# Moving the load of query 0's first 24 keys from SyncE's DMA queue to ScalarE's in a decode attention and GLU kernel

## The chip, the cores and the metric

One core of one Trainium2 chip. The metric is the device time of one execution in microseconds (us); the kernel before took 1301.58 us (median of three runs, 1301.52 to 1301.68). All data is float32.

## The reference, cut to what matters

```python
B, Sq, D = 2, 1, 448;  H, Sk, Dh = 16, 8192, 256;  F = 1792
q = (layernorm(x) @ wq).reshape(B, Sq, H, Dh).transpose(0, 2, 1, 3)
scores = einsum("bhqd,bhkd->bhqk", q, k_cache) * Dh ** -0.5
o = einsum("bhqk,bhkd->bhqd", softmax(scores), v_cache)
h = x + o.transpose(0, 2, 1, 3).reshape(B, Sq, H * Dh) @ wo
n = layernorm(h)
out = h + ((n @ w_gate) * (n @ w_up)) @ w_down
```

There is one new token for each of two batch rows, and 16 heads, so 32 queries; each has its own 8192 keys and 8192 values of 256 numbers, 8 MB each. The caches are some 537 MB of the 561 MB that the kernel reads: each byte of them is used once.

## The kernel before, in words

**Tiles.** A query's 8192 keys lie as 128 partitions by 64 keys by 256 numbers; a partition's 64 keys are 64 KB in one piece of memory. One buffer, `k_sb`, holds 2 x 64 - 16 = 112 keys a partition: even queries use its keys 0 to 63, odd ones 48 to 111 (`k_base`, line 276), so that 16 keys are shared ground. `v_sb` holds one query's values (64 a partition).

**Scores on VectorE.** `scores` (line 451) multiplies a part of the keys by the query, spread over all partitions, with one `tensor_mul` in place in `k_sb`, and sums over the 256 numbers with one `tensor_reduce`. Query 0 comes in two parts (`FIRST`, line 22): first the keys 40 to 63 of each partition, 24 of them, then the keys 0 to 39. The product of query 0's first part alone is written to `v_sb` instead of in place (lines 458 and 459). So keys 48 to 63 of `k_sb`, which query 1's keys overwrite, are free as soon as that product is done, and `v_sb` is free for query 0's values when its reduction is done. Queries after that take a part of 16 keys and one of 48.

**The rest of a query.** `top` and `softmax` take the largest score, the exponentials (ScalarE) and their sum; `mix` multiplies the values by the probabilities on TensorE as they land, and the results run through `wo` into `acc_ps`. After 32 queries come the second layernorm and the GLU, whose weights are loaded over `k_sb`.

**The start.** ScalarE issues the load of x (line 264) on its own DMA queue. SyncE issues all other loads of the kernel on its queue, in program order: the weights of the first head pair (`load_w`, line 303, 896 KB), the 24 keys (3072 KB) and the 40 keys (5120 KB) of query 0 (lines 304 and 305). Then, inside the loop over queries from line 612 on: query 1's keys (8192 KB), which wait for the product of the 24 keys; query 0's values, which wait for the reduction of the 24 keys; query 2's keys, which wait for query 1's first part; the next weights, and so on, keys and values in turn. VectorE and TensorE meanwhile do the layernorm of x, and TensorE then computes the first two heads' queries for both batch rows from the first weights (lines 389 to 402): four groups of four matmuls, each copied by ScalarE into `qs`. The first group is what query 0 needs.

**How orders and waits arise.** `Orders` collects the instructions of each engine in the order of the program. `load` (line 163) and `put` work out for each what it has to wait for, from the regions read and written, and `write` (line 201) emits the waits (`wait_ge`) and the instruction, with a semaphore that counts it. An engine runs its list in order, so a load that waits holds up the loads behind it on the same engine. In the profile, line 176 is that of every load, 229 that of every compute instruction, and 183 a wait of TensorE's.

Of the kernel before, what the change touches and what calls it, by code (L numbers as in the profile page):

```python
# [16 lines left out]
NJ = SK // P  # L17
# [4 lines left out]
FIRST = ((NJ - AHEAD, NJ), (0, NJ - AHEAD))  # L22
# [193 lines left out]
def decode_block(nc, x, k_cache, v_cache, w, wg, wu, wd, out):  # L216
# [31 lines left out]
    buffers = {"k": k_sb, "v": v_sb}  # L248
# [17 lines left out]
    def keys(cache, i, lo, hi):  # L266
        h, b = divmod(i, B)
        return cache[b, h].rearrange("(p j) d -> p j d", p=P)[:, lo:hi, :]

    def load_keys(name, cache, i, lo, hi, buf, at, event=None):  # L270
        o.load(
            "SP", name, buffers[buf][:, at : at + hi - lo, :], keys(cache, i, lo, hi),
            writes=[(buf, at * DH, (at + hi - lo) * DH)], event=event,
        )

    def k_base(i):
        return i % 2 * (NJ - OVER)

    def load_k(i, lo=0, hi=NJ):
        load_keys(f"d_k_{i}_{lo}", k_cache, i, lo, hi, "k", k_base(i) + lo)  # L280

    def v_parts(i):
        got, lo = [], 0
# [6 lines left out]
    def load_v(i, part):  # L290
        lo, hi, buf, at = part
        load_keys(f"d_v_{i}_{lo}", v_cache, i, lo, hi, buf, at, "e_v" if i < LOOP else None)

    def load_w(name, k, lo, hi, event=None):
        o.load("SP", name, w_sb[:, lo:hi], w[k][:, lo:hi], writes=[("w", lo, hi)], event=event)
# [5 lines left out]
        return 2 * WQ + h % 4 * WO  # L301

    load_w("d_w0", 0, 0, WQ)
    for lo, hi in FIRST:
        load_k(0, lo, hi)

    ident = sb("ident", P, P)
    put("POOL", "memset", ident, 0.0, w=["ident"])
# [77 lines left out]
    def q_at(h):  # L386
        return h % 2 * (1 + h // 2 % 2)

    for k in range(2):
        for b in range(B):  # L390
            for c in range(DC):
                at = c * 2 * DH + (k * DH if c < DC - 1 else 0)
# [5 lines left out]
            at = q_at(k)  # L398
# [213 lines left out]
    for n in range(NQ + 1):  # L612
        hp, at = divmod(n, 2 * B)
# [11 lines left out]
        if n + 1 < NQ:  # L625
            load_k(n + 1)
        for part in parts[1:]:
            load_v(n - 1, part)
        if n % 8 == 1:
            k = n // 8 + 1  # L630
# [35 lines left out]
    at = 0  # L666
# [191 lines left out]
```

## Time and profile before

| what | value |
|---|---|
| time, median of three runs | 1301.58 us |
| span of the profiled execution, first to last instruction | 1300.5 us |
| what lies around the span, against that median | 1.1 us |
| VectorE busy | 1130.8 us, 87% |
| TensorE busy | 488.8 us, 38% |
| ScalarE busy | 62.6 us, 5% |

The profiled execution has no time of its own listed beside its span; 1.1 us is the median less the span.

In the rows of the timeline the columns are start and duration in us, the engine, the line in the kernel, the operation, what it writes and reads, how many instructions are merged in the row, and in brackets the idle time before it and what ended that. A row with SPq or ACTq is the issue of a load by SyncE or ScalarE: its duration is that of the issue, not of the transfer. The list of DMA issues gives for each load its size and the time from its issue to its landing. In the list of DMA queues, q1 carries what SyncE issued, and q10 what ScalarE issued (x, the only load of that engine).

### The profile page before, as it was taken

The numbers are of one execution on the slowest core, as the hardware profiler recorded it, in microseconds if no ns is written. First come the engines' busy times: TensorE is split into PE (matmuls) and PEld (weight loads), VectorE is DVE, ScalarE is ACT, GpSimd is POOL, SyncE is SP. The second block draws the span as 40 slices with busy tenths as digits, with TensorE's granted clock in tenths as the row PEclk, the third lists the DMA queues.
The fourth block names the chain that finished last, engine by engine and source line by source line (L and its number), as shares of the span: only waits on it lengthen the run. The fifth ranks groups of instructions, "written<-read, shape, count | busy, mean of one in ns | idle before, by whom it ended". The sixth has DMA issues, their size and how long they took to land.

```text
span 1300.5 us, 6955 instructions
## 1 busy us (share of the span) xinstructions
PE 488.8 (38%) x2972; PEld 168.9 (13%) x2972; DVE 1130.8 (87%) x275; ACT 62.6 (5%) x184; POOL 1.4 (0%) x9
## 2 busy tenths in 40 slices
PE   3035422363331633215343063432424334243368
PEld 2011100120100201002101021010111001010113
DVE  7996988888988689888889868898888897889991
ACT  1000000000000000000000000000000000000000
POOL 0000000000000000000000000000000000000000
PEclk8566756686656766558666576665766667666578
DMA  9999999999999999999999999999999999999998
GB/s 414 423 434 448 424 437 431 427 441 423 448 424 435 448 423 443 427 439 429 435 435 423 433 448 423 448 424 443 427 443 427 423 436 445 426 438 429 435 433 374
DMA packets 12111, 561.45 MB, mean 432 GB/s; under 512 B 1602, under 2 KB 1732, under 8 KB 1988
## 3 DMA queue, kind: packets, MB, share of 16 engines
q1 hardware_dynamic: 12096, 561.30, 99.8%
q8 instruction: 6, 0.10, 0.0%
q14 instruction: 5, 0.04, 0.0%
q10 hardware_dynamic: 4, 0.00, 0.0%
HBM read 561.19 MB, written 0.11 MB: 432 GB/s over the span
## 4 chain that ended last, share of the span: by engine, by line
DMA 70%; DVE 29%; PE 0%; issue 0%; SPq 0%
DMA k_sb<-in_A_k_cache_dram 68%; DVE k_sb L229 14%; DVE s L229 14%; DMA k_sb<-in_wd_dram 2%; DVE nm L229 0%; PE y_ps L229 0%; SPq L176 0%; DVE m L229 0%; PE sm L229 0%; DVE v_sb L229 0%; DVE rl L229 0%
## 5 line engine op out<-in xcount | busy, mean ns | idle before, releaser
L229 DVE TENSOR_TENSOR k_sb<-k_sb,q 128x12288 f32<-128x12288 f32 (+2 forms) x67 | 549.6, 8203 | 130.3 <-DMA k_sb<-in_A_k_cache_dram 130.3
L229 DVE TENSOR_REDUCE s<-k_sb 128x48 f32<-128x12288 f32 (+2 forms) x67 | 549.3, 8198 | 0.2
L229 PE MATMUL o_ps<-v_sb,p 128*2 128x512 f32 x2000 | 288.2, 739 | 397.7 <-PEq L183 387.6
L229 PEld LDWEIGHTS o_ps<-v_sb,p 128*2 128x2 f32 x2000 | 53.7, 97 | 603.8 <-issue 591.3
L229 PE MATMUL sm<-nm,ones 1*128 1x1 f32 x64 | 16.6, 326 | 191.7 <-PEq L183 175.1
L229 PE MATMUL sm<-ident,m 128*1 128x128 f32 x32 | 10.9, 341 | 137.0 <-PEq L183 106.1
L229 PE MATMUL q_ps<-w_sb,xb 128*128 128x256 f32 (+1 forms) x172 | 59.3, 503 | 0.0
L229 ACT ACTIVATE o_sb<-o_ps 128x512 f32<-128x512 f32 x32 | 19.1, 597 | 703.9 <-PE o_ps L229 703.9
L229 PE MATMUL sm<-sel,o_sb 128*128 128x1 f32 x256 | 33.7, 253 | 25.8 <-PEq L183 22.9
L229 PE MATMUL acc_ps<-w_sb,oT 128*2 128x448 f32 x60 | 36.6, 749 | 15.9 <-PEq L183 11.0
L229 PEld LDWEIGHTS sm<-nm,ones 1*128 1x128 f32 x64 | 14.6, 283 | 201.2 <-issue 183.5
L229 PEld LDWEIGHTS sm<-sel,o_sb 128*128 128x128 f32 x256 | 31.8, 195 | 55.6 <-issue 48.2
L229 PEld LDWEIGHTS q_ps<-w_sb,xb 128*128 128x128 f32 x172 | 33.7, 200 | 30.0 <-issue 27.6
L229 PE MATMUL sm<-lsum,ones 128*128 128x1 f32 x64 | 17.5, 342 | 26.0 <-PEq L183 23.1
L229 ACT ACTIVATE nb<-sm 128x1 f32<-128x1 f32 x32 | 5.5, 171 | 395.7 <-PE sm L229 395.7
L229 PEld LDWEIGHTS sm<-ident,m 128*1 128x1 f32 x32 | 2.6, 81 | 149.8 <-issue 115.3
L229 PEld LDWEIGHTS sm<-lsum,ones 128*128 128x128 f32 x64 | 15.6, 303 | 28.0 <-issue 24.7
L229 ACT ACTIVATE q<-q_ps,rstd 128x512 f32<-128x512 f32 (+1 forms) x18 | 11.5, 640 | 71.9 <-PE q_ps L229 71.9
L229 PE MATMUL o_ps<-k_sb,p 128*2 128x512 f32 x48 | 9.3, 934 | 6.1 <-DMA k_sb<-in_A_v_cache_dram 6.1
L229 ACT ACTIVATE p<-s,nb 128x64 f32<-128x64 f32 x32 | 11.1, 347 | 1.0
L229 DVE TENSOR_TENSOR v_sb<-k_sb,q 128x6144 f32<-128x6144 f32 x1 | 6.6, 6557 | 4.8 <-DMA k_sb<-in_A_k_cache_dram 4.8
L229 PE MATMUL q_ps<-k_sb,xr 128*32 128x256 f32 (+3 forms) x96 | 10.0, 506 | 1.6 <-DMA k_sb<-in_B_w_gate_dram 1.6
(79 smaller groups left out, 85.1 us busy)
## 6 DMA issues: line engine op xcount, KB each, us to landing
v_sb<-in_A_v_cache_dram SPq DMA_DIRECT2D x4, 4096.0 KB, 30.5
w_sb<-in_w_dram SPq DMA_DIRECT2D x3, 3584.0 KB, 37.8
v_sb<-in_A_v_cache_dram SPq DMA_DIRECT2D x1, 6144.0 KB, 24.3
k_sb<-in_A_k_cache_dram SPq DMA_DIRECT2D x1, 5120.0 KB, 24.6
v_sb<-in_A_v_cache_dram SPq DMA_DIRECT2D x2, 2048.0 KB, 27.3
k_sb<-in_A_v_cache_dram SPq DMA_DIRECT2D x1, 4096.0 KB, 35.3
k_sb<-in_B_w_gate_dram SPq DMA_DIRECT2D x1, 3136.0 KB, 32.4
k_sb<-in_A_k_cache_dram SPq DMA_DIRECT2D x1, 3072.0 KB, 11.6
```

Of the source, the lines that this page charges most:

```text
L229: o.put(engine, lambda: f(*args, **kw), r, w, mark, event)
```

## The change

The load of the 24 keys is issued by ScalarE, right behind the load of x and ahead of everything else on that engine; the load of the 40 keys stays on SyncE's queue, now right behind the first weights. All waits, regions and sizes stay as they were, and so do all other loads.

```diff
-    def load_keys(name, cache, i, lo, hi, buf, at, event=None):
+    def load_keys(name, cache, i, lo, hi, buf, at, event=None, by="SP"):
         o.load(
-            "SP", name, buffers[buf][:, at : at + hi - lo, :], keys(cache, i, lo, hi),
+            by, name, buffers[buf][:, at : at + hi - lo, :], keys(cache, i, lo, hi),
             writes=[(buf, at * DH, (at + hi - lo) * DH)], event=event,
         )
...
-    def load_k(i, lo=0, hi=NJ):
-        load_keys(f"d_k_{i}_{lo}", k_cache, i, lo, hi, "k", k_base(i) + lo)
+    def load_k(i, lo=0, hi=NJ, by="SP"):
+        load_keys(f"d_k_{i}_{lo}", k_cache, i, lo, hi, "k", k_base(i) + lo, by=by)
...
     load_w("d_w0", 0, 0, WQ)
-    for lo, hi in FIRST:
-        load_k(0, lo, hi)
+    load_k(0, *FIRST[0], by="ACT")
+    load_k(0, *FIRST[1])
```

## The prediction

> **What bounds the kernel now.** I read the page first: busy shares, DMA queues, the chain's summary.
>
> ```profile
> span 1300.5 us, 6955 instructions
> ...
> q1 hardware_dynamic: 12096, 561.30, 99.8%
> ...
> q10 hardware_dynamic: 4, 0.00, 0.0%
> ...
> DMA 70%; DVE 29%; PE 0%; issue 0%; SPq 0%
> ```
>
> The last row puts 70% of the chain on DMA and 29% on VectorE, but the queue row decides: SyncE's packets occupy the 16 DMA engines for 99.8% of the span. The DMA engines are the bound; VectorE appears in the chain because a load is issued when VectorE frees a buffer, while older loads still keep the engines busy. The table by stretches gives the rate, and the start.
>
> ```profile
> core 0: us, PE busy (x) PEld busy (x) DVE busy (x) ACT busy (x) POOL busy (x), PEclk, DMA share, GB/s
> 1.00:2.00 1.00, 0.00 (x0) 0.00 (x0) 0.48 (x4) 0.70 (x1) 0.84 (x4) 1.00 0.55 90
> 2.00:3.00 1.00, 0.01 (x1) 0.01 (x1) 0.88 (x3) 0.58 (x1) 0.14 (x1) 1.00 0.71 165
> 100.00:300.00 200.00, 77.82 (x437) 26.61 (x437) 173.15 (x36) 10.11 (x29) 0.00 (x0) 0.67 1.01 435
> ```
>
> A steady stretch moves 435 GB/s at a share of 1.01. So a change to the order of loads can gain only what is idle in the first 3 us, and can lose only by letting the engines run dry. The question is whether anything in the first 60 us makes a load come too late for that. Here is the timeline of that stretch.
>
> ```profile
> 0.73 0.53 ACTq L176 DMA_DIRECT2D v_sb<-in_A_x_dram  x1
> ...
> 0.73 0.38 SPq L176 DMA_DIRECT2D w_sb<-in_w_dram  x1
> ...
> 1.17 18.57 SPq L176 DMA_DIRECT2D k_sb<-in_A_k_cache_dram  x3
> ...
> 1.30 1.28 ACT L229 ACT_TABLE_LOAD   x1 [1.30 <-PEq L839]
> ...
> 7.30 9.25 PE L229 MATMUL q_ps<-w_sb,xb 128*128 128x256 f32 x32
> ...
> 11.10 0.47 ACT L229 ACTIVATE q<-q_ps,rstd 128x256 f32<-128x256 f32 x1 [1.85 <-PE q_ps L229]
> 12.83 6.56 DVE L229 TENSOR_TENSOR v_sb<-k_sb,q 128x6144 f32<-128x6144 f32 x1 [4.83 <-DMA k_sb<-in_A_k_cache_dram]
> ...
> 19.42 6.55 DVE L229 TENSOR_REDUCE s<-v_sb 128x24 f32<-128x6144 f32 x1
> 26.07 0.33 SPq L176 DMA_DIRECT2D v_sb<-in_A_v_cache_dram  x1
> 26.24 10.82 DVE L229 TENSOR_TENSOR k_sb<-k_sb,q 128x10240 f32<-128x10240 f32 x1 [0.27 <-DMA k_sb<-in_A_k_cache_dram]
> ...
> 57.05 0.33 SPq L176 DMA_DIRECT2D k_sb<-in_A_k_cache_dram  x1
> ```
>
> The DMA issues of the same stretch (size, us to landing), then one line of the view of the key buffer for the first 30 us, then an issue from the kernel's end:
>
> ```profile
> k_sb<-in_A_k_cache_dram SPq DMA_DIRECT2D x1, 5120.0 KB, 24.6
> ...
> k_sb<-in_A_k_cache_dram SPq DMA_DIRECT2D x1, 3072.0 KB, 11.6
> w_sb<-in_w_dram SPq DMA_DIRECT2D x1, 896.0 KB, 4.8
> ...
> v_sb<-in_A_v_cache_dram SPq DMA_DIRECT2D x1, 38.8
> ```
>
> ```profile
> L176 SPq DMA_DIRECT2D k_sb<-in_A_k_cache_dram x3: 328/422/423, 1.2 to 19.4; - x3
> ```
>
> ```profile
> out_dram<-v_sb SPq DMA_DIRECT2D x1, 56.0 KB, 1.6
> ```
>
> Landings: the first weights at 0.73 + 4.8 = 5.5, the 24 keys at 1.17 + 11.6 = 12.8. VectorE starts their product at 12.83; the query was ready at 11.10 + 0.47 = 11.57, so the keys were last. The product ends at 19.4, and there query 1's keys are issued, the third of the three issues. The reduction ends at 26.0, where query 0's values are issued and the 40 keys are needed; those land at about 26.2.
>
> **What the change moves.** One issue leaves SyncE: it took up to 0.42 us there (the issues of 1.2 to 19.4 took 328 to 423 ns). The 40 keys are issued at 1.17 in its place, some 0.45 us sooner; worth nothing, since their bytes stand behind the first weights. On ScalarE the new issue follows x: 0.73 + 0.53 + a step of 0.06 as on SyncE (0.73 + 0.38 to 1.17), so at about 1.3, and ends by 1.8. What it delays there is the table load of 1.28 us at 1.30, now ending near 3.1; ScalarE's next work is an activation on the variance behind TensorE's small sums, just ahead of 7.30. Cost nothing, with 4 us of cover.
>
> The real effect: the 24 keys no longer stand behind the first weights, but share the engines with whatever SyncE has queued. The bytes are the same. Engines began at about 1.45 (share 0.55 of the second microsecond), 0.7 us after the first issue; so the 24 keys' first bytes come at 1.3 + 0.7 = 2.0. By then the weights have moved 90 GB/s x 1 us = 0.09 of 0.92 MB: seven of the eight rows that each engine carries (128 rows, 16 engines) are still to go.
>
> How two queues share an engine is shown nowhere before: q10 carries four packets. I bound it. Row times: the 24 keys' 3072 KB took 12.8 - 5.5 = 7.3 us, so a 24 KB row takes 0.91 us of its engine, a 7 KB row of weights 0.27, a 40 KB row 1.51. If the engine takes the two queues row about, the weights' seven rows each wait for a row of keys: they land at 5.5 + 7 x 0.91 = 11.9, and the keys at 12.8 to 14.3 (the same bytes before them, and at most one 40 KB row). If the first weights went whole, and the keys then alternated with the 40 KB rows, they would land at 5.5 + 8 x (0.91 + 1.51) = 24.9, or one 40 KB row less, 23.4. I take row about with the weights, because seven rows are left at 2.0.
>
> Then the query comes last, not the keys: TensorE took 11.57 - 7.30 = 4.3 us from its first matmul to the query's copy, and now begins at 11.9 instead of 7.30. Query 0's first product starts at T = 16.2, later by d = 3.4 us than 12.83.
>
> What d costs. (1) Query 1's keys are issued at T + 6.6. The engines have work until the 40 keys are through: 12.8 + 12.1 (5120 KB at 435 GB/s) = 24.9 as a landing, less the time between last byte and landing. The output's 56 KB took 1.6 us in all, 0.7 of it before the first byte and 0.1 for the bytes, which leaves 0.8; so they run dry at 24.1. With 0.7 us from issue to first byte, the issue must come by 23.4, so T by 16.8 and d by 4.0: the cost is **d - 4.0 us, and nothing below that**. A d of 3.4 fits with 0.6 us to spare. As engines don't end together (the 40 keys land 1.3 us past 24.9), the early ones may lose some tenths; I take 0.1.
>
> (2) VectorE itself runs d - 0.27 late from 26.24 on (it waited 0.27 there). Query 2's keys go out at 57.05 + 3.1 = 60.2; query 0's values keep the engines busy until 26.07 + 38.8 = 64.9, less 0.8: 3.2 us to spare after 0.7 for the first byte. (3) What is left of the delay is waited out further on:
>
> ```profile
> 84.17 4.43 DVE L229 TENSOR_TENSOR k_sb<-k_sb,q 128x4096 f32<-128x4096 f32 x1 [1.04 <-DMA k_sb<-in_A_k_cache_dram]
> ...
> 131.25 4.43 DVE L229 TENSOR_TENSOR k_sb<-k_sb,q 128x4096 f32<-128x4096 f32 x1 [12.04 <-DMA k_sb<-in_A_k_cache_dram]
> ```
>
> VectorE takes back 1.04 us at 84.17 and the rest in the 12.04 us in front of 131.25, where it waits for a transfer in any case. From there on nothing differs.
>
> A gain is bounded too: between 1 and 3 us the engines are busy for 0.55 and 0.71 of the time, and the third microsecond moves 165 instead of 435 GB/s. A second queue could fill part of that from 2.0 on: (435 - 165) / 435 = 0.6 us at most. So the sum for this edit lies between -0.6 and the rivals' bounds below, and I take +0.1: 1300.6 against the span of 1300.5, which is 1301.7 on the median's scale (the 1.1 us around the span are not touched).
>
> [...]
>
> **The rivals.** *Order unchanged.* An engine finishes its whole share of a load before it turns to the other queue: weights, the 24 keys, the 40 keys, as before; T = 12.83 and 1301.6. For it: each load has nine packets on an engine (12096 packets over SyncE's 84 loads are 144, so 128 rows and one more on each of 16 engines), which may go as a unit; no row here shows two queues at work. [...]
>
> *Equal bytes.* Engines share finely: the 24 keys get half of 435 GB/s and land at 2.0 + 14.5 + 0.8 = 17.3. The weights land early, so T = 17.3, d = 4.5, cost 0.5 us, up to 1.1 for engines that end early: 1302.1 to 1302.7.
>
> *The 24 keys lose to the 40* (slower). If the weights are mostly through, because the second issue on ScalarE starts late or its queue is served late, the 24 keys alternate with 40 KB rows: landing 23.4 to 24.9, d = 10.6 to 12.1, cost 6.6 to 8.1: 1308 to 1310. If all the 40 KB rows go first, T = 26.2, d = 13.4, and 1311. It decides from a cost of 2.6 us, so d = 6.6 and T = 19.4: that takes (19.4 - 12.8) / 1.51 = 4.4 such rows ahead of the keys' last one. Against it: the two issues lie 0.6 us apart, and seven of the weights' rows are left. A table load of 1.28 us ahead of the issue would still leave about five.
>
> **How the numbers follow.** Row about: 0.54, 1301.7. Order unchanged: 0.11. Equal bytes or a few more 40 KB rows, costs of 0.5 to 2.6 us: 0.17. Keys behind the 40: 0.16. Something faster than the bound of 0.6 allows: 0.02. A measurement of this kernel tells 0.2%, 2.6 us, from no change; so faster 0.02, same 0.82, slower 0.16. The range runs from the largest gain, 1301.0, to 1304.2, which takes in the first three cases.
>
> **What would show it.** In the changed profile: ACTq with a second issue at about 1.3; TensorE's first matmul on the weights near 12 instead of 7.30; VectorE's first product near 16, the issue of query 1's keys near 23; the reduction's end near 29 and VectorE a few us late until its long wait ahead of 131; landings from then on as before. If the first product starts at 12.8, the order is unchanged; at 17 to 18 with matmuls from 7.3, bytes are shared. It is wrong if that product starts past 19 and the DMA row shows a hole near 25.

## The result, and the profile after

The changed kernel takes 1312.28 us (median of five runs, 1312.08 to 1313.19) against 1301.52 (1301.33 to 1301.68): a ratio of 1.0084, 95% interval 1.0073 to 1.0094, so 10.8 us slower. The prediction was no change, 1301.7 in a range of 1301.0 to 1304.2: wrong. What came is its slower rival, "the 24 keys lose to the 40", priced at 1308 to 1311.

From the page of the changed kernel: the span, the DMA share in 40 slices, and two queues (packets, MB, share of the 16 engines' span).

```profile
span 1311.9 us, 6955 instructions
...
DMA  6999999999999999999999999999999999999998
...
q1 hardware_dynamic: 11952, 558.16, 98.4%
q10 hardware_dynamic: 148, 3.15, 0.6%
```

All that is lost lies in the first slice, a 6 where there was a 9. ScalarE's queue now carries 148 packets: the four of x and 144 of the 24 keys. The start's timeline in the changed kernel, then its DMA issues of the first 60 us:

```profile
1.17 32.55 SPq L176 DMA_DIRECT2D k_sb<-in_A_k_cache_dram  x2
1.32 0.36 ACTq L176 DMA_DIRECT2D k_sb<-in_A_k_cache_dram  x1
...
1.71 1.28 ACT L229 ACT_TABLE_LOAD   x1 [1.71 <-PEq L839]
...
7.28 9.46 PE L229 MATMUL q_ps<-w_sb,xb 128*128 128x256 f32 x32
...
26.80 6.56 DVE L229 TENSOR_TENSOR v_sb<-k_sb,q 128x6144 f32<-128x6144 f32 x1 [18.82 <-DMA k_sb<-in_A_k_cache_dram]
...
40.04 0.33 SPq L176 DMA_DIRECT2D v_sb<-in_A_v_cache_dram  x1
...
70.66 0.33 SPq L176 DMA_DIRECT2D k_sb<-in_A_k_cache_dram  x1
```

```profile
k_sb<-in_A_k_cache_dram SPq DMA_DIRECT2D x1, 5120.0 KB, 25.3
k_sb<-in_A_k_cache_dram ACTq DMA_DIRECT2D x1, 3072.0 KB, 25.4
w_sb<-in_w_dram SPq DMA_DIRECT2D x1, 896.0 KB, 4.9
...
k_sb<-in_A_k_cache_dram SPq DMA_DIRECT2D x1, 21.8
```

The second issue on ScalarE comes at 1.32, as forecast. But the first weights still land at 0.73 + 4.9 = 5.6, and TensorE starts on them at 7.28 as before: they did not share with the keys. The 24 keys land at 1.32 + 25.4 = 26.7 instead of 12.8, and query 0's first product starts 14.0 us late. Below is which queue moved what, for 2.0 to 5.6 us, then for 6 to 6.9 and for 6.9 to 8.4, then for 6 to 24 us as a whole. A row is one partition's piece of a load. Each row is one packet here, counted in the stretch in which it starts. Each load but the tiny one of x has one more packet, of under 512 B, on each of the 16 DMA engines (144 packets for the 128 rows of the 24 keys); it is read here as the signal that the load has landed there, since in the kernel a load counts its semaphore up by 16.

```profile
q1 hardware_dynamic: 149, 1.49, 103.7%
```

```profile
q10 hardware_dynamic: 16, 0.39, 101.3%
```

```profile
q1 hardware_dynamic: 16, 0.66, 100.9%
```

```profile
q1 hardware_dynamic: 116, 4.59, 58.9%
q10 hardware_dynamic: 131, 3.12, 40.4%
```

Between 2.0 and 5.6 us nothing of ScalarE's queue moves, though the keys were issued at 1.32: SyncE's 149 packets are the rest of the weights' rows, their 16 signals, and one 40 KB row on each engine. The 24 keys' first rows start at 6.0 to 6.8, when these are done. From then on each of the 16 engines takes one row of each queue in turn: sixteen rows of 24 KB (0.39 MB), sixteen of 40 KB (0.66 MB), and so on, some 112 of 40 KB and 127 of 24 KB up to 24 us. It is row about, but with the wrong partner. At 24.5 us fifteen engines are through with both loads; the sixteenth still has a row of the 24 keys, from 25.1 to 26.0, and the landing at 26.7 waits for it. Here is all that starts between 24.5 and 34.3 us:

```profile
q10 hardware_dynamic: 2, 0.02, 0.6%
q1 hardware_dynamic: 1, 0.00, 0.0%
```

So the engines run dry, as the table by stretches shows, first of the kernel before, then of the changed one:

```profile
25.00:33.00 8.00, 0.00 (x0) 0.00 (x0) 7.73 (x2) 0.00 (x0) 0.00 (x0) 0.50 0.93 401
...
40.00:1290.00 1250.00, 469.22 (x2758) 154.71 (x2762) 1097.93 (x247) 57.36 (x176) 0.00 (x0) 0.65 1.00 433
```

```profile
25.00:33.00 8.00, 0.00 (x0) 0.00 (x0) 6.20 (x1) 0.00 (x0) 0.00 (x0) 0.50 0.01 3
...
40.00:1290.00 1250.00, 459.92 (x2675) 151.07 (x2675) 1109.08 (x235) 56.51 (x173) 0.00 (x0) 0.65 1.00 434
```

Between 25 and 33 us DMA is busy for 0.01 of the time (3 GB/s instead of 401): both loads of query 0 are through but for that one row, and query 1's keys can't be issued before the late product has ended at 33.4. From 40 us on the two kernels move the same 433 to 434 GB/s. The loss is that one hole.

### The profile page after: what moved, and what is told of

Same layout as the page of the kernel before. It is cut to its first block, busy times and chain, and to the rows that moved or that the text cites. A ratio compares the mean times of both kernels' runs of the same rounds, so it can differ in the third digit from the quotient of the medians.

```text
span 1311.9 us, 6955 instructions
## 1 busy us (share of the span) xinstructions
PE 488.6 (37%) x2972; PEld 170.2 (13%) x2972; DVE 1130.6 (86%) x275; ACT 62.7 (5%) x184; POOL 1.4 (0%) x9
## 4 chain that ended last, share of the span: by engine, by line
DMA 68%; DVE 32%; PE 0%; issue 0%; ACTq 0%; SPq 0%; DVEq 0%
DMA k_sb<-in_A_k_cache_dram 65%; DVE s L229 16%; DVE k_sb L229 15%; DMA k_sb<-in_wd_dram 2%; DVE v_sb L229 1%; DVE nm L229 0%; PE y_ps L229 0%; DVE m L229 0%; ACTq L176 0%; DVE rl L229 0%; PE sm L229 0%; SPq L176 0%; DVEq L209 0%
## 5 line engine op out<-in xcount | busy, mean ns | idle before, releaser
L229 PE MATMUL o_ps<-v_sb,p 128*2 128x512 f32 x2000 | 291.6, 745 | 391.5 <-PEq L183 381.3
L229 PE MATMUL sm<-sel,o_sb 128*128 128x1 f32 x256 | 33.7, 253 | 25.8 <-PEq L183 22.9
L229 PE MATMUL acc_ps<-w_sb,oT 128*2 128x448 f32 x60 | 34.5, 712 | 15.7 <-PEq L183 10.9
L229 PEld LDWEIGHTS sm<-lsum,ones 128*128 128x128 f32 x64 | 15.9, 308 | 28.0 <-issue 24.7
L229 ACT ACTIVATE oT<-sm,rl 128x2 f32<-128x2 f32 x32 | 8.4, 262 | 39.1 <-PE sm L229 39.1
## 6 DMA issues: line engine op xcount, KB each, us to landing
v_sb<-in_A_v_cache_dram SPq DMA_DIRECT2D x2, 2048.0 KB, 26.2
k_sb<-in_A_k_cache_dram ACTq DMA_DIRECT2D x1, 3072.0 KB, 25.4
```

Source lines behind the costliest of these rows:

```text
L229: o.put(engine, lambda: f(*args, **kw), r, w, mark, event)
```

## The experiments

Two questions: why the 24 keys ran with the 40 keys and not with the weights, and whether their lateness alone costs the 10.8 us. T is the start of query 0's first product, d its delay against 12.83. Three theories of the sharing went into the first four runs: **taken ahead** (an engine commits itself to rows in order of arrival, about ten ahead of the one it moves, an estimate from the changed kernel, where seven rows of weights, their signal and a 40 KB row went ahead of the 24 keys; only rows beyond that go in turn), **late queue** (ScalarE's queue is served late or after SyncE's), and the prediction's **row about from arrival**. The edits of these four are against the changed kernel.

**Keys first.** x goes to the head of SyncE's queue, so that the 24 keys are ScalarE's first issue.

```diff
-    o.load("ACT", "d_x", x_sb[:, :D], ...
+    o.load("SP", "d_x", x_sb[:, :D], ...
```

> The load of x goes to the head of SyncE's queue, and the load of the 24 keys is the first issue of ScalarE, at 0.73 us. Theory 'taken ahead' (each DMA engine takes rows in order of arrival, about ten ahead of those it moves, and only rows not yet taken go in turn between the queues): the eight rows of the 24 keys are all taken before the first weights arrive some 0.4 us later, so the keys land near 1.4 + 8 x 0.91 + 0.8 = 9.5 and the weights after them near 11.8; query 0's first product starts near 16 (the query comes last), a delay of 3.3 us against the kernel before, which costs nothing: 1301.5, at most 1302.5. Theory 'late queue' (ScalarE's queue is served late or behind SyncE's): weights at 5 to 6, keys in turn with the 40 KB rows, first product at 24 to 27, 1308 to 1312. Theory 'row about from arrival' (the prediction's): weights and keys both land near 12, first product near 16, 1301.5 to 1302.

Measured: 1303.05 (ratio 1.0013, 1.0003 to 1.0023). The DMA issues, then the first product:

```profile
k_sb<-in_A_k_cache_dram ACTq DMA_DIRECT2D x1, 3072.0 KB, 11.2
w_sb<-in_w_dram SPq DMA_DIRECT2D x1, 896.0 KB, 11.3
```

```profile
16.67 6.56 DVE L229 TENSOR_TENSOR v_sb<-k_sb,q 128x6144 f32<-128x6144 f32 x1 [8.67 <-ACT q L229]
```

The keys land at 0.73 + 11.2 = 11.9 and the weights, issued at 1.14, at 12.4: the two share, and the query comes last, at T = 16.67. That is the picture the prediction drew for the changed kernel, had by 0.4 us of order of arrival. "Late queue" falls here: ScalarE's rows run ahead. But "taken ahead" is too large at ten rows: all eight key rows would have landed by 9.5. Only the first three on each engine ran alone: between 1.9 and 4.5 us one completion packet was all that SyncE's queue got through. Then the two go row about, 80 packets against 79 from 4.7 to 10.8 us. The time is above what either theory had (1301.5 to 1302.5): a d of 3.84 us, under the prediction's cover of 4.0, costs 1.6 us.

```profile
q10 hardware_dynamic: 41, 1.01, 99.4%
q1 hardware_dynamic: 1, 0.00, 0.0%
```

**Both on ScalarE.**

```diff
-    load_k(0, *FIRST[1])
+    load_k(0, *FIRST[1], by="ACT")
```

> Both key loads of query 0 are issued by ScalarE behind x, the 24 keys first; SyncE keeps the rest. 'Taken ahead': weights at 5.5, 24 keys at 12.8 to 13, first product at 12.8 to 13; query 1's keys, issued by SyncE near 19.5, find the last rows of the 40 keys already taken, so the 40 keys land near 26 and the time is 1301.5 (at most 1302). 'Row about from arrival': weights near 11.9, first product near 16; query 1's 64 KB rows go in turn with the last rows of the 40 keys from about 23 on, 40 keys at 27 to 30, 1301.5 to 1303. 'Late queue': first 24-key row not before 5.7, first product near 13.8, and the 40 keys behind query 1's keys: landing at 35 or later, VectorE some 9 us or more late, 1304 or more.

Measured: 1303.04 (1301.5 to 1303.8; ratio 1.0010, 1.0000 to 1.0020). The interval doesn't tell this from no change; the profiled execution is the one of 1303.80 us. T is 12.78, against 12.83 in the kernel before: one queue behind the other's weights kept the old order, and ScalarE's queue was as good as SyncE's. But the 40 keys are needed at 25.9 and land only at 30.9, as the bracket shows; they share their last rows with query 1's keys, which SyncE issued at 19.37.

```profile
30.88 10.83 DVE L229 TENSOR_TENSOR k_sb<-k_sb,q 128x10240 f32<-128x10240 f32 x1 [4.95 <-DMA k_sb<-in_A_k_cache_dram]
```

VectorE is late by 4.6 us at query 2's keys (issued at 61.68 instead of 57.05), and the engines run short there: 1.31 between 62 and 64 us and 0.68 between 64 and 68 in this profile, 0.89 in the mean. "Taken ahead" in the strength of ten rows (landing near 26) falls again. "Row about from arrival" comes near in this landing (27 to 30), but falls by T, which it put near 16.

**Forty wait.** SyncE issues the 40 keys only when the first weights have landed.

```diff
-    load_k(0, *FIRST[1])
+    load_k(0, *FIRST[1], after=[("w", 0, WQ)])
...
```

The lines left out hand `after`, a new argument, to the load as what it reads, so that its issue waits for the landing of the weights.

> As the changed kernel, but SyncE waits for the landing of the first weights (about 5.5) before it issues the 40 keys. 'Taken ahead': the weights land at 5.5, the 24 keys' rows are all taken by then and move first; 24 keys at 12.8 to 13.5, first product at the same time, 1301.5 to 1302. 'Late queue': the 24 keys' first row comes near 5.7 and the 40 keys arrive near 6.2, then in turn: 24 keys at 21 to 25, 1306 to 1311. 'Row about from arrival': the weights land near 11.7 and only then are the 40 keys issued; the 24 keys land near 12.5, first product near 16, 1301.5 to 1302.

Measured: 1305.02 (ratio 1.0027, 1.0017 to 1.0038), T = 18.66: no theory's number. The 40 keys go out at 5.26. Three stretches of this run tell what happened, 5.9 to 9.0 us, 15.9 to 17.7 us and 17.75 to 18.25 us:

```profile
q10 hardware_dynamic: 48, 1.18, 88.3%
```

```profile
q1 hardware_dynamic: 16, 0.66, 84.1%
```

```profile
q1 hardware_dynamic: 16, 0.66, 302.8%
q10 hardware_dynamic: 16, 0.00, 1.8%
```

No row of the 40 keys starts before 9.0, 3.8 us after their issue; from 5.9 on each engine starts three more 24 KB rows first. So rows are taken ahead, but three of 24 KB, not ten. The second and third stretch are a surprise: the last rows of the 24 keys have started by 15.8 and end by 16.7, and what is left of ScalarE's queue are 16 packets of under 512 B, one for each engine, the signals of its landing. One 40 KB row on each engine (16 packets, 0.66 MB) goes ahead of them; the next sixteen start right behind them. The signal stood in line like a row, and the keys counted as landed only at 1.30 + 17.3 = 18.6, 1.9 us after the last row's end.

**Swap.** The 24 keys back on SyncE, the 40 on ScalarE.

```diff
-    load_k(0, *FIRST[0], by="ACT")
-    load_k(0, *FIRST[1])
+    load_k(0, *FIRST[0])
+    load_k(0, *FIRST[1], by="ACT")
```

> The 24 keys go back to SyncE's queue behind the first weights, and the 40 keys are issued by ScalarE behind x instead. 'Taken ahead', with rows in turn between the two queues whichever of them is ScalarE's: weights at 5.5, then one or two rows of the 24 keys ahead and the rest in turn with 40 KB rows: 24 keys near 23 to 24, first product near 23.5, a delay of 10.7 us, 1308 to 1309. 'Late queue': the 24 keys run ahead of all that ScalarE has issued and land at 12.8 as in the kernel before, 1301.5. 'Row about from arrival': the weights in turn with 40 KB rows, landing near 16; the 24 keys later than 23, 1308 to 1311.

Measured: 1312.32 (ratio 1.0083, 1.0066 to 1.0100), T = 26.39: the changed kernel's loss with the engines' roles exchanged.

```profile
26.39 6.56 DVE L229 TENSOR_TENSOR v_sb<-k_sb,q 128x6144 f32<-128x6144 f32 x1 [18.40 <-DMA k_sb<-in_A_k_cache_dram]
```

So it isn't ScalarE's queue; it is that the two loads stand on two queues at all. The size was low by 3 us. About half of it is the signal's place in the line, which was not in it: the 24 keys' rows end by 23.0, and a 40 KB row goes ahead of the signal on each engine, up to 24.5. The rest is mostly one engine, whose signal comes 1.3 us after the others', at 25.8.

The next three runs test the price of lateness, and a look-ahead put, from the runs so far, at 2.2 to 2.9 us of transfers in place of ten rows.

**Late by 14, one queue.** The kernel before, with fills by VectorE ahead of the first product.

```diff
     act(std, std, AF.Exp, scale=0.0, r=["std"], w=["std"])
+    for _ in range(3):
+        dve("memset", v_sb[:, :23, :], 0.0, w=[("v", 0, 23 * DH)])
```

> The kernel before, all loads on SyncE, with three fills of v_sb by VectorE (5888 numbers a partition each, some 6.2 us) put ahead of query 0's first product: nothing but that product is late, to about 26.6. Theory 'hole' (the loss is only that query 1's keys are issued too late, so that the DMA engines run dry from about 24 to 34): the same loss as the changed kernel at the same start, delay less 2.8 us: 1312 for a start at 26.6, with DMA idle from 25 to 33. Rival 'sharing costs' (two queues at work lose bandwidth on the engines): clearly less, 1306 or below, since only one queue is used.

Measured: 1312.64 (ratio 1.0086, 1.0069 to 1.0103). The product, and DMA in the stretch of the hole:

```profile
26.73 6.56 DVE L229 TENSOR_TENSOR v_sb<-k_sb,q 128x6144 f32<-128x6144 f32 x1
```

```profile
25.00:33.00 8.00, 1.65 (x2) 0.08 (x2) 7.89 (x3) 0.00 (x0) 0.00 (x0) 0.50 0.01 2
```

With all loads on SyncE and in the old order, the same late product makes the same hole and the same loss. Two queues at work cost no bandwidth that shows (429 GB/s from 6 to 24 us in the changed kernel, 431 in the kernel before); the late start is all of it. Here all 16 engines send the 40 keys' signal between 23.8 and 24.4. Query 1's keys are issued at 33.31, and their first rows, one on each engine, start at 34.3 to 35.0. The stretch from 34.2 to 35.2 us:

```profile
q1 hardware_dynamic: 16, 1.05, 304.5%
```

Sixteen packets that fill 304.5% of 1 us on 16 engines took 3.05 us in the mean; in the kernel before, where these rows follow others without a gap, one of 64 KB takes 2.42 (32 of them fill 107.5% of 28 to 32.5 us).

**Late by 3.** One fill, of 29 keys' room.

```diff
     act(std, std, AF.Exp, scale=0.0, r=["std"], w=["std"])
+    dve("memset", v_sb[:, :29, :], 0.0, w=[("v", 0, 29 * DH)])
```

> As the one above with one fill of 7424 numbers (some 7.8 us), so that query 0's first product starts near 15.9, 3.1 us late. Theory 'hole' with the threshold read from the runs so far (cost = delay - 2.8): 0.2 to 0.5 us, 1301.5 to 1302. With the prediction's threshold of 4.0: no change, 1301.4. If any delay of VectorE cost in full: 1304.5.

Measured: 1301.84 (ratio 1.0003, 0.9994 to 1.0013) with T = 16.08: +0.4 us, no difference that this comparison tells from none, and in the middle of the 0.2 to 0.5 expected. Costs against the kernel before in the same comparison, by d:

| run | T, us | d, us | cost, us | d - cost |
|---|---|---|---|---|
| late by 3 | 16.08 | 3.25 | 0.4 | 2.8 |
| keys first | 16.67 | 3.84 | 1.6 | 2.2 |
| forty wait | 18.66 | 5.83 | 3.6 | 2.2 |
| swap | 26.39 | 13.56 | 10.9 | 2.7 |
| late by 14 | 26.73 | 13.90 | 11.2 | 2.7 |
| changed | 26.80 | 13.97 | 10.8 | 3.2 |

Whatever made the product late in these six runs, the time grew by its delay less 2.2 to 3.2 us. The small costs are less sure than the large: that of "late by 3" lies within the noise.

**Forty late.** The changed kernel, with the 40 keys issued only when ScalarE's activation on `std` has ended.

```diff
-    load_k(0, *FIRST[1])
...
     act(std, std, AF.Exp, scale=0.0, r=["std"], w=["std"])
+    load_k(0, *FIRST[1], after=["std"])
```

> As the changed kernel, but SyncE issues the 40 keys only behind ScalarE's activation that ends near 9.25 (the second on std). Theory 'taken ahead', with about 2.2 to 2.9 us of transfers taken ahead on each engine: at 9.9, when the 40 keys arrive, the 24 keys' last 2.1 us are already taken; they land at 12.8 to 13, first product at 12.8 to 13, no hole since the 40 keys' rows are there before 12: 1301.5. Rival 'rows in turn from arrival': two or three rows of 24 keys are left at 9.9, each behind a 40 KB row: 24 keys at 15.5 to 17.5, 1301.5 to 1303.

Measured: 1302.11 (1301.51 to 1302.78; ratio 1.0006, 0.9996 to 1.0015), T = 12.85. The 40 keys' issue, then the product:

```profile
9.27 10.49 SPq L176 DMA_DIRECT2D k_sb<-in_A_k_cache_dram  x2
```

```profile
12.85 6.56 DVE L229 TENSOR_TENSOR v_sb<-k_sb,q 128x6144 f32<-128x6144 f32 x1 [4.86 <-DMA k_sb<-in_A_k_cache_dram]
```

The 24 keys are still on ScalarE's queue, the 40 on SyncE's, and 10 of the 10.8 us are back, only because the 40 keys arrive when the other load's last 2 us have been taken. In turn from arrival was expected to give a T of 15.5 or more. The profiled execution is the one of 1301.51 us; T in the others is not known. A fixed delay of whichever queue comes second, the other reading of the runs so far, doesn't fit: the 40 keys' first row starts 2.5 us after its issue here and 3.8 us in "forty wait", each time behind the rows that were in line. So in these runs the look-ahead decided which loads went in turn. No run here is faster than the kernel before; its engines, with SyncE's packets on them for 99.8% of the span, have no hole to fill.

## Why the prediction was wrong

**The step that failed** is "I take row about with the weights, because seven rows are left at 2.0". Seven rows of weights had not moved by then, but the engines had already taken them, and one 40 KB row behind them. So the 24 keys' first row came at 6.0 instead of 2.0, and the partner in the turns was the 40 keys: 1.51 us a turn instead of 0.27. The prediction weighed the count of rows not yet moved; what counted is how much stood in line at arrival. Where another load was in line, the first row of the second queue's load started 3.4 to 4.7 us after its issue, against 1.0 us for the first weights, which had an idle engine: 3.4 in "keys first" (the weights, issued at 1.14, had no row under way by 4.5), 3.8 in "forty wait" (24 KB rows ahead), 4.7 in the changed kernel (the weights' rows and a 40 KB row); 2.5 in "forty late", where only some 2 us of the other load were left. Less that 1.0, and that last run aside, some 2.4 to 3.7 us of transfers were taken ahead. In rows of one engine that is three in "forty wait" and some nine in the changed kernel, so it was no fixed number of rows; whether bytes or time set it was not tried apart.

**Row about** itself was right: between 6.0 and 8.4 us of the changed kernel sixteen rows of 24 KB start, one for each engine, then sixteen of 40 KB. The rival "order unchanged", with a whole load as the unit, is refuted by the same rows.

**The landing** of a load was taken as its last byte plus 0.8 us. In the kernel before it is 0.4 for the 24 keys (last row's end at 12.4, landing at 12.8). With a second queue at work it came later: 1.9 us in "forty wait", where a 40 KB row of the other queue started on each engine ahead of the signal.

**The cost of lateness** was right in kind (the delay less a cover, by query 1's late issue) and its cover of 4.0 us too large: 2.2 to 3.2. The time at which the engines run dry, 24.1, was right (23.8 to 24.4 in "late by 14"). Two other terms were not. From issue to first byte the sum has 0.7 us, read from the share of the second microsecond; but in the kernel before no packet starts before 1.6, and the first weights' rows start 1.0 us after their issue. Query 1's keys took 0.95 to 1.6 us after the hole. And a first row took 3.05 us in the mean after the hole of "late by 14" instead of 2.42, which the sum doesn't have. 4.0 less 0.3 to 0.9, less 0.6, is 2.5 to 3.1.

**The spread of the engines.** The prediction put the 40 keys' landing, 1.3 us past its sum, down to engines that don't end together. It is one engine alone: in the kernel before, fifteen send the 40 keys' signal by 24.5 us and the last at 25.7. In the seven runs in which a packet of 16 KB of another queue (q8, "instruction", some 0.9 us) starts between 21 and 23 us, one engine is 1.0 to 1.6 us behind the rest; where that packet comes after the 40 keys' last rows have started ("keys first", 23.8, and "late by 14", 27.7), all end within 0.6 us. That the packet holds up that engine is read from these times; no run moves it on purpose.

**Right were** the issue at 1.3, the table load's free delay (1.30 to 1.71, nothing late behind it), that no gain was to be had, and that nothing is lost after the start (434 GB/s from 40 us on). The second check, at query 2's keys, did no harm in the changed kernel, where the hole had moved query 0's values back as well; it is the one that cost in "both on ScalarE", where the cover was short too.

The rival's price came near, in part by luck: row about with 40 KB rows from the weights' end gave 23.4 to 24.9 for the landing, "all of the 40 first" 26.2 and 1311. Fifteen engines ran as the first of these has it, with eight 40 KB rows ahead of the last 24 KB row, and sent their signals by 24.5. The landing came at 26.7 because of the sixteenth engine, and the time at 1312.28 because the cover was shorter too. The rival was given 0.16, on the strength of the seven rows.

## What to carry to other kernels

In these runs one queue kept its order, and on it a small load that must land first was safe behind the loads that it needs and ahead of those that it doesn't: in the kernel before, T was 12.83. On a second queue the 24 keys traded rows with the first queue's 40 keys as far as the two were not yet in line when they met: T was 26.80 in the changed kernel, 18.66 in "forty wait", and 12.85 in "forty late", where the last 24 KB rows were in line when the 40 keys came. Where engines are busy all the time, as here for 99.8% of the span, look for the load whose issue hangs on the late step, and for how much is in line at that moment: here 2.2 to 3.2 us of cover, and what lay past it was paid in full (10.8 us for a delay of 13.97). When two queues meet, compare times of arrival and what is in line by then, not how much has moved: seven of the weights' eight rows had not moved at 2.0, and yet the 24 keys' first row started at 6.0.

## What the runs showed of the hardware that had not been expected

In these runs the DMA engines took some 2.4 to 3.7 us of transfers ahead in order of arrival (first rows of the second queue 3.4 to 4.7 us after their issue instead of 1.0); two queues alternated row by row, with unequal rows too (sixteen of 24 KB, then sixteen of 40 KB in the changed kernel); and the packet that signals a landing waited its turn as a row does (1.9 us instead of 0.4 in "forty wait"). After an idle stretch the first 64 KB rows took 3.05 us in the mean instead of 2.42 ("late by 14"). A load landed with its slowest engine (the 24 keys at 26.7 in the changed kernel, where fifteen engines were through by 24.5), and one engine of sixteen was 1.0 to 1.6 us behind with query 0's keys in seven of nine profiles.
